# Two tiles of 256 tokens handed out with the sixth chunk, in a fused convolution and mixture-of-experts kernel

## The chip, the core and the metric

The kernel runs on one core of one Trainium2 chip. Its time is the device time of one execution in microseconds; the kernel before has a median of 1246.07 us over three runs (1243.16 to 1247.38). The profile comes from one more execution of the same program. TensorE (PE) multiplies matrices, VectorE (DVE) and ScalarE (ACT) work elementwise, GpSimd (POOL) computes a little and issues the indirect transfers, SyncE (SP) issues the other transfers. Each engine works through its own list of instructions in the order in which the program wrote them.

## The reference

```python
# x: (8, 3584, 192), weight_gen: (8, 3584, 8, 7)
w = softmax(weight_gen, over the last axis)           # 7 taps per token and head
x_unf[b, s, k] = x_pad[b, s + k]                      # 6 rows of zeros ahead of each sequence
out = einsum('bshk,bskhg->bshg', w, x_unf)            # a causal convolution, 8 heads of 24
# out as 28672 tokens of 192
logits = out @ w_gate                                 # 8 experts
e = argmax(logits); gate = softmax(logits)[e]
y = gate * (maximum(out @ w1[e], 0.0) @ w2[e])        # 192 -> 1024 -> 192, of one expert
```

Every token goes through the convolution, then through the one expert with the highest logit.

## The kernel before

The 28672 tokens are cut into 28 chunks of 1024, counted from 0 (`NCH`, `J * P`). For each chunk VectorE forms the convolution (`taps`, L354 and L378, fourteen passes over 128x1536); the result is split into a 16-bit high part (ScalarE, L448) and its residual (VectorE, `low`, L461 to L467). TensorE transposes the parts (L473), ScalarE copies them out (L475), TensorE forms the logits (`logits`, L485), VectorE the arg max and the gate (`route1`, `gate`), TensorE counts ranks (`ranks`, L512 and L514), VectorE turns them into places in eight queues in device memory, one per expert (`places`, L535 to L544), and POOL scatters the chunk's rows there with eight indirect transfers (`send`, L559). After the last chunk `pad_queues` scatters eight more, of padding rows. Behind a chunk, `choose` runs `select` (L573 to L605, on VectorE, one partition) for each event of the plan: it picks the experts whose queues are longest and writes the first rows of the tiles to be run.

A tile is T rows of one expert's queue. SP fetches it (`fetch`): its rows, transposed (`xt`, L743), all weights of its expert (`wt`, L745, 1796 KB, three buffers before the last chunk's tiles) and its gates (`meta`, L748). A tile's `xt` waits until its chunk's rows are in the queue; where the fetch stands in the program behind `pad_queues`, its `xt` waits for the padding rows too. On TensorE a tile is 8 blocks of the hidden layer, five matmuls each (L805, T columns wide; `fg` blocks in a group, two where T is 256, one where it is 384), and then for each 128 tokens 24 matmuls of the second layer (L711, 192 columns). Between the two the hidden values are split into `hh` and its residual `hl`. That goes one of two ways (L811): with ScalarE alone and a matmul that subtracts (L814, L818, L820), or with ScalarE and VectorE (L825, L828). A tile's second layer is written into the next tile's groups (`second`, `prev`).

What is handed out after which chunk is fixed when the program is written. `t_main` gives the sizes of tile for a chunk: nothing after chunk 0, 256 after chunks 1 to 4 (`EARLY` is 5), 384 after that, and 384, 256 and 128 after the last one. `make_plan` adds 1024 to `pending` with each chunk and hands out a tile of T while `pending > E * (T - 1)`, that is while some expert must have T rows in its queue. Before, that gives 1, 4, 4 and 4 tiles of 256 after chunks 1 to 4, none after chunk 5, three of 384 after chunk 6, two after chunk 7, three after chunk 8, three after chunk 9, two after chunk 10 and so on in this pattern, and after chunk 27 three of 384, three of 256 and 22 of 128 and fewer.

The order of the instructions is written by a planner with two clocks of its own, `clock[0]` for VectorE and `clock[1]` for TensorE. `vector_step` appends VectorE's next piece (a residual, a step of a chunk's routing, of its split, of the convolution) while VectorE's clock is behind TensorE's; then the next group of a tile is appended. A tile is not begun before its selection stands in the list, and TensorE's clock is put to at least `FETCH` = 16 after it (L977). With a chunk's split, its transposes go to TensorE's list at that place.

Of the kernel before, what the change touches and what calls it, by code (L numbers as in the profile page):

```python
# [20 lines left out]
E = 8  # L21
# [13 lines left out]
EARLY = 5  # L35
# [17 lines left out]
T_MAIN = 384  # L53
# [18 lines left out]


def t_main(c, last):
    if c < 1:
        return []
    if c < EARLY:
        return [256]
    if c < last:
        return [T_MAIN]  # L80
    return [T_MAIN, 256, 128]


def make_plan(n_chunks, chunk):


    events, pending = [], 0

    def full(ev, T):
        nonlocal pending  # L90
        s = 0
        while pending > E * (T - 1):
            pending -= T
            s += 1
        if s:
            ev.append((T, s, None))

    for c in range(n_chunks):
        pending += chunk
        ev = []  # L100
        for T in t_main(c, n_chunks - 1):
            full(ev, T)
        events.append(ev)


    T = 128
    n = (pending + E * (T - 1)) // T
    ends = [min(T, pending // k if k <= E else (pending - T * (k - E)) // E) for k in range(1, n + 1)]
    events[-1].append((T, n, [-(-m // T_STEP) * T_STEP for m in ends]))
    return events  # L110
# [3 lines left out]
def conv_moe_kernel(ctx: ExitStack, tc: tile.TileContext, x, wgen, w_gate, w1, w2, out):  # L114
# [4 lines left out]
    NCH = NP // J  # L119
# [488 lines left out]
    todo = []  # L608
# [109 lines left out]
    def fetch(n):  # L718
        T, rows, i, c, _ = todo[n]

        def rows_of(ins):


            for later in range(c + 1, sent[0] + 1):
                tc.declare_no_dep(ins.ins, group=f"s{later}", reason="the rows read were written by earlier chunks")
            for names in writers[:c + 1]:
                for name in names:
                    tc.add_manual_dep(ins.ins, name, wait_for, reason="may have written the rows read")
            tc.add_to_no_dep_group("qr", ins.ins)

        r = nc.sync.value_load(rows[0:1, i:i + 1], min_val=0, max_val=E * NCAP - 512)
        e = nc.s_assert_within(r >> 15, 0, E - 1,
                               skip_runtime_bounds_check_because="a row of queue e lies in [e * NCAP, (e + 1) * NCAP)")
        late = c == NCH - 1
        if late and not lates:

            conv_pools.close()
            lates.append(ctx.enter_context(tc.tile_pool(name="late", bufs=AHEAD, side="right", reuse_waits="tile")))
            lates.append(n)
        ring = late and (n - lates[1]) % (AHEAD + 3) < AHEAD  # L740
        px, pw = (lates[0], lates[0]) if ring else (ffx, ffw)
        xt = px.tile([P, 3, T_MAIN], F16, name="xt", bufs=AHEAD if ring else 3)
        rows_of(nc.sync.dma_start_transpose(xt[:, :, 0:T], q16[ds(r, T), 0:2 * D]))  # L743
        wt = pw.tile([P, WROW], F16, name="wt")
        nc.sync.dma_start(wt, wq[ds(e * P, P), :])  # L745
        meta = px.tile([P, 4, 2], F32, name="meta", bufs=AHEAD + 1 if ring else 4)
        p = min(P, T)
        rows_of(nc.sync.dma_start(meta[0:p, 0:T // p, :], q32[ds(r, T), D:D + 2].rearrange("(s p) c -> p s c", p=p)))  # L748
        return T, xt, wt, meta
# [4 lines left out]
    def experts():  # L754
# [8 lines left out]
        n = 0  # L763

        def second(m):
            while m > 0:
                r = next(prev, 0)
                if r == 0:
                    break
                if r is None:  # L770
                    m -= 1
                else:
                    outs.append(r)

        def flush():
            while outs:
                idx, o = outs.pop(0)
                scatter(out, idx, o, "o", bound=N - 1)

        while True:  # L780
            go = yield n, 0.0
            if not go:
                break
            while len(done_) < min(n + 2, len(todo)):
                loaded[len(done_)] = fetch(len(done_))
                done_.append(len(done_))
            T, xt, wt, meta = loaded.pop(n)

            fac = ffx.tile([P, 4], F32, name="fac", bufs=1)
            hh = ffh.tile([P, NF, T], F16, name="hh", padded_shape=[P, NF, T_MAIN])  # L790
            hl = ffh.tile([P, NF, T], F16, name="hl", padded_shape=[P, NF, T_MAIN])
            fg = max(g for g in (1, 2, 4, 8) if g * T <= 512 or g == 1)
            groups = NF // fg
            for t in range(groups):
                if t:
                    yield None, 0.0
                f0 = t * fg
                flush()
                while len(pend) > 3:
                    low_part()  # L800
                ph = ps_h.tile([P, fg, T], F32, name="ph")
                for g in range(fg):
                    f = f0 + g
                    for k, (wc, xc) in enumerate(((0, 0), (0, 2), (O_L0, 0), (O_H1, 1), (O_L1, 1))):
                        nc.tensor.matmul(ph[:, g], wt[:, wc + f * P:wc + (f + 1) * P], xt[:, xc, 0:T],  # L805
                                         start=(k == 0 and g == 0), stop=(k == 4),
                                         skip_group_check=g > 0)
                hv, lv = hh[:, f0:f0 + fg], hl[:, f0:f0 + fg]
                while subs:
                    subs.pop(0)()  # L810
                if (n % 3 == 1 or todo[n][3] < EARLY) and todo[n][3] < NCH - 1:  # L811


                    nc.scalar.activation(hv, ph, AF.Relu, scale=SHRINK)  # L814

                    def rest(ph=ph, hv=hv, lv=lv, fg=fg):
                        for g in range(fg):
                            nc.tensor.matmul(ph[:, g], negi, hv[:, g], start=False, stop=True,  # L818
                                             skip_group_check=True)
                        nc.scalar.activation(lv, ph, AF.Relu)  # L820

                    subs.append(rest)
                    clock[1] += T * fg * (6 + 4.5) / 2400.0 + 15 * fg * MM
                else:
                    nc.scalar.activation(hv, ph, AF.Relu)  # L825

                    def lo(ph=ph, hv=hv, lv=lv):
                        nc.vector.scalar_tensor_tensor(lv, ph, 0.0, hv, op0=ALU.max, op1=ALU.subtract)  # L828
                        return (T * fg + 60) / 960.0

                    cost = T * fg * (5 + 4.5) / 2400.0 + 14 * fg * MM
                    clock[1] += cost
                    pend.append((clock[1] + LATE, n, lo))
                if t > 0 or groups == 1:
                    while pend and pend[0][1] < n:
                        low_part()
                    m = -(-left // (groups - t))
                    second(m)
                    left -= m
                if t == groups - 1:  # L840
                    p = min(P, T)
                    nc.scalar.activation(fac[0:p, 0:T // p], meta[0:p, 0:T // p, 0], AF.Copy,
                                         scale=wt[0:p, O_INV:O_INV + 2].bitcast(F32))
                if t >= 1 and len(done_) < len(todo):
                    m = len(done_)
                    if m <= n + 2 or (todo[m][3] == NCH - 1 and m <= n + AHEAD + 2):
                        loaded[m] = fetch(m)
                        done_.append(m)
            while subs:
                subs.pop(0)()  # L850
            second(10 ** 6)
            prev = l2(T, hh, hl, wt, meta, fac)
            left = -(-T // P) * NF * 3
            n += 1
# [4 lines left out]


    plan = make_plan(NCH, J * P)
    clock = [0.0, 0.0]

    def low_part():
        at, _, lo = pend.pop(0)
        clock[0] = max(clock[0], at) + lo()
# [93 lines left out]
    with tc.manual_schedule(engines={mybir.EngineType.DVE}):  # L960
# [6 lines left out]
        n, _ = next(parts)  # L967
        while n is not None or parts is not None:
# [11 lines left out]
            n, _ = parts.send(True)  # L980
# [23 lines left out]
```

## Time and profile before

| | |
|---|---|
| median of three runs | 1246.07 us (1243.16 to 1247.38) |
| the profiled execution | 1242.18 us, span 1240.5 us |
| TensorE busy | 1133.4 us (91%), granted clock 0.965 |
| VectorE busy | 1036.7 us (84%) |
| ScalarE busy | 696.8 us (56%) |
| GpSimd busy | 660.6 us (53%) |
| weight loads (wt) | 97 of 1796 KB |
| read from and written to device memory | 239 GB/s over the span |

The busy times are means over stages that differ: up to about 175 us the expert weights are prepared and the first chunks run, then tiles and chunks go side by side until about 1020 us, and after that there are only tiles. So a stretch of the span tells more than the whole.

### The profile page before, as it was taken

How to read it: one execution, taken by the hardware profiler on the slowest of the kernel's cores; microseconds unless marked ns; L12 is line 12 of the kernel's file. 1: busy time of each engine (PE TensorE's matmuls, PEld its weight loads, DVE VectorE, ACT ScalarE, POOL GpSimd, SP SyncE). 2: the span in 40 equal slices, each digit the busy share in tenths (PEclk: the TensorE clock that was granted, in tenths of full speed). 3: DMA queues.
4: the chain of work that ended last, by engine and by line, in shares of the span. 5: the costliest groups of instructions: out<-in, count | busy, mean ns of one | idle time of the engine just before them, and what ended most of it. 6: DMA issues, size and time to landing. Idle time of an engine off the chain costs nothing.

```text
span 1240.5 us, 30087 instructions
## 1 busy us (share of the span) xinstructions
PE 1133.4 (91%) x11621; PEld 927.2 (75%) x11621; DVE 1036.7 (84%) x1849; ACT 696.8 (56%) x1459; POOL 660.6 (53%) x562
## 2 busy tenths in 40 slices
PE   5692189997999999999999999999999998999997
PEld 3461179896678788778788787787777786789997
DVE  7999966999999999999999999999998976232331
ACT  3455167675566666656756666656655663543442
POOL 6850853666656565446755565656464656222222
PEclk9896599999999999999999999999999999999998
DMA  9996698897768878787798878878776667999995
GB/s 277 346 323 241 232 282 264 287 304 236 232 201 267 265 230 250 238 234 235 247 277 237 237 227 255 247 240 254 239 215 178 191 197 222 340 348 348 321 362 218
DMA packets 185133, 320.93 MB, mean 259 GB/s; under 512 B 132752, under 2 KB 156434, under 8 KB 169118
## 3 DMA queue, kind: packets, MB, share of 16 engines
q1 hardware_dynamic: 162862, 273.68, 70.8%
q0 software_dynamic: 22128, 45.33, 11.1%
q8 instruction: 91, 1.49, 0.5%
q14 instruction: 52, 0.43, 0.1%
HBM read 236.17 MB, written 60.76 MB: 239 GB/s over the span
## 4 chain that ended last, share of the span: by engine, by line
PE 63%; DVE 13%; DMA 10%; issue 7%; POOL 4%; SPq 1%; ACT 1%; POOLq 0%; DVEq 0%; ACTq 0%
PE ph L805 29%; PE y L711 27%; DVE tv L354 4%; DVE acc L378 3%; DMA wt<-wq 3%; PE ph L473 2%; PE ph L818 2%; DMA f<-in_moe_w_dram 2%; POOL out_dram L559 2%; DMA xt<-queue 2%; DMA queue<-pl,pos 2%; DVE hl L828 1%; POOL queue L559 1%; PE ph L363 1%; PE pm L485 1%
## 5 line engine op out<-in xcount | busy, mean ns | idle before, releaser
L805 PE MATMUL ph<-xt,wt 128*128 128x384 f16 (+6 forms) x3880 | 578.8, 292 | 24.5 <-DMA wt<-wq 16.8
L711 PE MATMUL y<-wt,hh 128*128 128x192 f16 (+2 forms) x3696 | 504.5, 247 | 2.1 <-ACT o L715 2.1
L559 POOL DMA_INDIRECT out_dram<-o,meta x231 | 288.5, 1249 | 394.6 <-ACT o L715 349.0
L711 PE MATMUL y<-wt,hl 128*128 128x192 f16 (+2 forms) x1848 | 450.3, 247 | 0.4 <-ACT hl L820 0.2
L805 PEld LDWEIGHTS <-wt 128*128 128x128 f16 x3880 | 329.3, 98 | 144.4 <-DMA wt<-wq 18.9
L711 PEld LDWEIGHTS <-hh 128*128 128x128 f16 (+2 forms) x3696 | 337.0, 99 | 35.9 <-issue 5.0
L559 POOL DMA_INDIRECT queue<-pl,pos x224 | 286.8, 1280 | 118.1 <-issue 56.7
L828 DVE SCALAR_TENSOR_TENSOR hl<-ph,hh 128x384 f16<-128x384 f32 (+2 forms) x372 | 204.2, 562 | 144.2 <-ACT hh L825 139.0
L354 DVE TENSOR_TENSOR tv<-x_sb,wp 128x1536 f32<-128x1536 f32 (+1 forms) x171 | 289.0, 1693 | 3.9 <-PE ph L363 3.7
L825 ACT ACTIVATE hh<-ph 128x384 f16<-128x384 f32 (+2 forms) x372 | 185.5, 501 | 181.0 <-PE ph L805 170.4
L378 DVE TENSOR_TENSOR acc<-acc,tv 128x1536 f32<-128x1536 f32 x150 | 261.8, 1745 | 0.0
L711 PEld LDWEIGHTS <-hl 128*128 128x128 f16 (+2 forms) x1848 | 181.7, 98 | 16.5 <-ACT hl L820 1.4
L814 ACT ACTIVATE hh<-ph 128x384 f16<-128x384 f32 (+1 forms) x204 | 105.2, 518 | 84.7 <-PE ph L805 82.0
L715 ACT ACTIVATE o<-y,fac 128x192 f32<-128x192 f32 (+2 forms) x231 | 91.7, 418 | 89.4 <-PE y L711 83.4
L820 ACT ACTIVATE hl<-ph 128x384 f16<-128x384 f32 (+1 forms) x204 | 104.1, 519 | 37.0 <-PE ph L818 36.4
L475 ACT ACTIVATE xg<-ph 128x1024 f16<-128x1024 f16 x84 | 83.9, 1027 | 24.3 <-PE ph L473 24.2
L473 PE MATMUL ph<-idh,pl 128*128 128x128 f16 x672 | 56.1, 225 | 25.4 <-ACT pl L448 15.8
L818 PE MATMUL ph<-hh,negi 128*128 128x384 f16 (+1 forms) x256 | 68.1, 304 | 1.7 <-ACT hh L814 1.6
L473 PEld LDWEIGHTS <-pl 128*128 128x128 f16 x672 | 44.5, 101 | 29.4 <-ACT pl L448 16.1
L363 PE MATMUL ph<-tv,identf 128*128 128x384 f32 x126 | 51.6, 553 | 7.6 <-DVE tv L354 7.3
L413 ACT ACTIVATE junk<-x_sb 128x768 bf16<-128x768 f32 (+2 forms) x56 | 48.0, 857 | 13.6 <-DMA x_sb<-in_x_dram 6.5
L322 POOL TENSOR_TENSOR w_sb<-w_sb,mx 128x448 f32<-128x448 f32 x28 | 29.7, 1062 | 45.5 <-DVE mx L321 43.6
(121 smaller groups left out, 780.7 us busy)
## 6 DMA issues: line engine op xcount, KB each, us to landing
wt<-wq SPq DMA_DIRECT2D x97, 1796.0 KB
x_sb<-in_x_dram SPq DMA_DIRECT2D x27, 1344.0 KB
w_sb<-in_weight_gen_dram SPq DMA_DIRECT2D x28, 224.0 KB
wq<-ws SPq DMA_DIRECT2D x8, 772.0 KB
f<-in_moe_w_dram SPq DMA_DIRECT2D x8, 768.0 KB
f<-in_moe_w_dram SPq DMA_DIRECT2D x8, 512.0 KB
wq<-ws SPq DMA_DIRECT2D x8, 512.0 KB
wq<-ws SPq DMA_DIRECT2D x32, 128.0 KB
```

The source lines that it names most:

```text
L354: eng.tensor_tensor(out, xs, ws, op=ALU.mult)
L378: eng.tensor_tensor(ac, ac, t, op=ALU.add)
L473: nc.tensor.transpose(pt[:, m, :], p16[:, j, n * P:(n + 1) * P], idh)
L559: st = nc.gpsimd.indirect_dma_start(out=dst, out_offset=bass.IndirectOffsetOnAxis(ap=idx, axis=0), in_=src, in_offset=None, **kw)
L711: nc.tensor.matmul(y, hx[:, f, sl], w2v[:, f, t, :], start=(f == 0 and k == 0), stop=(f == NF - 1 and k == 2))
L715: nc.scalar.activation(o[0:m, :], y, AF.Copy, scale=fac[0:m, s:s + 1])
L805: nc.tensor.matmul(ph[:, g], wt[:, wc + f * P:wc + (f + 1) * P], xt[:, xc, 0:T], start=(k == 0 and g == 0), stop=(k == 4), skip_group_chec ...
L814: nc.scalar.activation(hv, ph, AF.Relu, scale=SHRINK)
L818: nc.tensor.matmul(ph[:, g], negi, hv[:, g], start=False, stop=True, skip_group_check=True)
L820: nc.scalar.activation(lv, ph, AF.Relu)
L825: nc.scalar.activation(hv, ph, AF.Relu)
L828: nc.vector.scalar_tensor_tensor(lv, ph, 0.0, hv, op0=ALU.max, op1=ALU.subtract)
```

## The change

Chunk 5 hands out at most two tiles of 256. `t_main` returns pairs of a size and the most tiles that may go out; the condition at L811 takes chunk 5's tiles along, so that both go the way with ScalarE alone.

```diff
     if c < EARLY:
-        return [256]
+        return [(256, 99)]
+    if c == EARLY:
+        return [(256, 2)]
     if c < last:
-        return [T_MAIN]
-    return [T_MAIN, 256, 128]
+        return [(T_MAIN, 99)]
+    return [(T_MAIN, 99), (256, 99), (128, 99)]
...
-    def full(ev, T):
+    def full(ev, T, most):
         nonlocal pending
         s = 0
-        while pending > E * (T - 1):
+        while s < most and pending > E * (T - 1):
             pending -= T
             s += 1
...
-        for T in t_main(c, n_chunks - 1):
-            full(ev, T)
+        for T, most in t_main(c, n_chunks - 1):
+            full(ev, T, most)
...
-                if (n % 3 == 1 or todo[n][3] < EARLY) and todo[n][3] < NCH - 1:
+                if (n % 3 == 1 or todo[n][3] <= EARLY) and todo[n][3] < NCH - 1:
```

## Rows read from the trace of the kernel before

**Rows 1.** Busy time by stretch (start:end, length, engines, granted clock, DMA share, GB/s).
```profile
287.70:296.40 8.70, 5.56 (x69) 4.95 (x67) 8.30 (x15) 4.65 (x11) 7.13 (x5) 1.00 0.55 174
296.40:303.00 6.60, 6.47 (x58) 4.48 (x58) 6.60 (x13) 3.98 (x10) 2.12 (x2) 1.00 0.97 321
303.00:317.00 14.00, 8.48 (x68) 5.50 (x69) 14.00 (x25) 6.72 (x10) 9.76 (x7) 0.63 1.06 318
317.00:331.30 14.30, 13.58 (x128) 10.52 (x126) 14.30 (x30) 8.44 (x21) 7.49 (x6) 1.00 0.50 151
331.30:345.70 14.40, 13.04 (x118) 10.15 (x117) 14.40 (x25) 7.24 (x16) 8.93 (x8) 1.00 0.83 253
345.70:650.00 304.30, 304.26 (x3037) 242.58 (x3035) 297.57 (x529) 191.85 (x418) 174.14 (x139) 1.00 0.79 244
...
1021.00:1048.30 27.30, 23.93 (x218) 18.82 (x216) 20.81 (x66) 10.74 (x25) 20.90 (x22) 1.00 0.66 219
1048.30:1240.50 192.20, 184.82 (x2312) 168.36 (x2312) 52.20 (x84) 78.96 (x176) 46.40 (x48) 0.97 0.96 320
```

**Rows 2.** Chain of waits, 215 to 345 us (start, length, what).
```profile
215.26 12.71 DMA wt<-wq
...
261.84 1.09 PE ph L805 x10
...
265.50 1.99 PE y L711 x24
...
268.58 7.53 DMA wt<-wq
...
288.39 1.67 DVE acc L378
...
334.52 0.48 DVE hl L828
335.04 0.97 PE ph L805 x5
...
341.16 2.44 PE ph L805 x15
```

**Rows 3.** Chain of waits, 1041 to 1050 us.
```profile
1041.61 2.41 DMA queue<-padrow,padi
1044.04 4.10 DMA xt<-queue
1048.28 1.99 PE ph L805 x8
```

**Rows 4.** Timeline of TensorE (start, length, line, tiles, shape, [idle before]).
```profile
296.36 1.14 PE L805 MATMUL ph<-xt,wt 128*128 128x384 f16 x6 [2.32 <-DMA xt<-queue]
...
306.37 0.29 PE L473 MATMUL ph<-idh,pl 128*128 128x128 f16 x1 [3.50 <-ACT pl L448]
...
345.75 0.98 PE L805 MATMUL ph<-xt,wt 128*128 128x384 f16 x5
...
529.76 0.61 PE L473 MATMUL ph<-idh,pl 128*128 128x128 f16 x8
```

**Rows 5.** Timeline of VectorE, end of chunk 14's split.
```profile
529.59 0.14 DVE L467 TENSOR_TENSOR lsc<-isx,nin 128x1 f32<-128x1 f32 x1
```

**Rows 6.** Timeline of SP's queue, 292 to 323 us.
```profile
292.95 1.35 SPq L743 DMA_TRANSPOSE xt<-queue  x1
...
322.17 1.31 SPq L743 DMA_TRANSPOSE xt<-queue  x1
```

**Rows 7.** Timeline of POOL, first of chunk 7's eight rows.
```profile
306.51 0.99 POOL L559 DMA_INDIRECT queue<-pl,pos  x1 [2.70 <-DVE pos L544]
```

**Rows 8.** Groups by line and shape (count, busy us, mean ns, idle before).
```profile
L828 DVE SCALAR_TENSOR_TENSOR hl<-ph,hh 128x384 f16<-128x384 f32 x323 | 171.5, 546 | 65.5 <-ACT hh L825 65.3
...
L584 DVE TENSOR_TENSOR eq<-cand,top 1x128 f32<-1x128 f32 x7 | 2.0, 280 | 0.0
```

## The prediction

> **What bounds the kernel now.** I read the table by stretches first [rows 1], then the chain of waits in order of time [rows 2, 3], then single engines' timelines where the chain changes hands [rows 4 to 7], and last the prices by shape [rows 8]. Chunks are counted from 0, so the sixth is chunk 5; tiles are counted from 0 too.
>
> From 345.7 to 650 us TensorE is busy for 304.26 of 304.30 us, and after 1048.3 it has the work alone (184.8 of 192.2 us, VectorE 52.2) [rows 1]. VectorE in the first of these stretches is idle for only 304.30 - 297.57 = 6.7 us. So the middle is bound by both engines at once, and the end by TensorE. The two are locked by one written order: chunk 14's residual is ready on VectorE at 529.73 (529.59 + 0.14), and its transposes start on TensorE at 529.76 [rows 4, 5]. TensorE cannot run ahead of VectorE there by more than the order has put ahead of such a point.
>
> The hole lies before that. Tiles 9 to 12 belong to chunk 4, chunk 5 hands out nothing, and tile 13 waits for chunk 6: its xt is issued at 292.95, its first matmul runs at 296.36 [rows 4, 6]. In the five stretches from 287.7 to 345.7 TensorE idles 3.14 + 0.13 + 5.52 + 0.72 + 1.36 = 10.9 us, and the granted clock is 0.63 in the third (303 to 317), so part of it ran at the 1.2 GHz level [rows 1]. But from 288.4 to 335.0 the chain goes through VectorE [rows 2], which is busy all 42.7 us of the stretches from 303 on [rows 1]. TensorE's hole is therefore not simply time of the end.
>
> There is a second hole at the end of the middle. Tile 67's xt waits for the last padding row of the queues (1041.61 + 2.41), lands, and TensorE starts at 1048.28; in that stretch it idles 27.30 - 23.93 = 3.4 us [rows 1, 3].
>
> **The change part by part.** *What the plan hands out.* Before a chunk, pending tokens are compared with 8*(T-1). Chunk 4 leaves 1792; chunk 5 makes that 2816, over 2040, so two tiles of 256 go out and 2304 are left. Chunk 6 then has 3328 and hands out one tile of 384 in place of three, chunk 7 three in place of two, chunk 8 three as before, chunk 9 two in place of three; from there the pattern 3, 3, 2 stands one chunk off. Tokens handed out by chunk 6: 256 fewer; by chunks 7 and 8: 128 more, and so on by turns. The last chunk gets two tiles of 384 and four of 256, where it had three and three. In all 98 tiles instead of 97.
>
> *Prices on TensorE.* A 256-wide matmul costs 1.09/10 = 0.109 us, a 384-wide one 2.44/15 = 0.163, one of the second layer 1.99/24 = 0.083 [rows 2]. A tile of 256 is 40 x 0.109 + 48 x 0.083 = 8.3 us, and 9.2 with the eight residual matmuls of the ScalarE path; a tile of 384 is 40 x 0.163 + 72 x 0.083 = 12.5, and 13.8 with them. The edited condition (<= EARLY) puts both new tiles on the ScalarE path. Two tiles of 384 become three of 256, the same columns; 120 x 0.109 - 80 x 0.163 is nothing, and the ScalarE path costs 2 x 0.9 for the new tiles, less 1.3, since 18 instead of 19 of the 384-wide tiles take it: +0.5 us.
>
> *Prices on VectorE.* Residuals by VectorE before the last chunk: 37 tiles, before and after, so none gained or lost. One selection more: nine instructions whose dearest is 280 ns [rows 8], about 2.0 us, less some 0.4 for chunk 6's, which picks one tile instead of three: +1.6 us, on the chain in that stretch. Against it, before chunk 9's transposes only one tile (15) has its residuals on VectorE where two (14, 15) had: 8 x 0.546 = 4.4 us later [rows 8]. So VectorE reaches that point 2.8 us sooner, and must make it up later, where it has the 6.7 us of idle time.
>
> *One weight load more* (1.8 MB) stands in the stretch from 276 to 298 us. Loads took 7.5 to 12.7 us to land [rows 2]. The new tile 13's can go when tile 10 is done with its buffer, near 276, and lands between 284 and 289, while TensorE is with tile 12 until 287.7: hidden, or 1 us late. The three loads after it come one per freed buffer; at 12.7 instead of 9.2 us they would cost up to 3.5 us each, at 7.5 nothing. I take 1 us in all, since the nearest row (268.58) took 7.5. Should the cover go, this is the rival below that ends slower. The Trainium skill, "DMA: Bandwidth & Descriptors", section "Issuing engines are not separate DMA queues", says that transfers of SP and POOL share the same engines and interleave. The rows bear it out: the DMA share is 1.06 in 303 to 317 [rows 1]. By that rule the added load is not free there: at 318 GB/s it takes 5.6 us of all engines, and if all of it delayed chunk 6's rows, the sum below would come to nothing.
>
> *Where the filled time goes.* After tile 12 the plan had 13.8 + 2 x 12.5 = 38.8 us of tiles to run before chunk 7's first; now 2 x 9.2 + 12.5 = 30.9, which is 7.9 us less. The hole is filled at chunk 6 and opens again at chunk 7. Chunk 7's first xt was issued at 322.17 and needs about 3.4 us (292.95 to 296.36) [rows 4, 6]; with the added selection that is 327. TensorE starts on the new tiles at 288; with 30.9 us of tiles and about 4 us of transposes, logits and the like (345.75 - 287.7, less 38.8 of tiles, 10.9 of idle and up to 4.2 that the low clock cost, below), it gets there near 323 and waits some 4 us. It then runs chunk 7's first tile at 327, where that started at 345.75 [rows 4]: 18.7 us sooner with 7.9 us less done, a lead of 11. But that lead meets chunk 9's transposes, which hang on VectorE. What is kept is only what the written order has placed ahead of such points, and that follows from the tokens: in the end 128 more before the padding rows, 128 fewer after them.
>
> *The sum at the end.* Behind the padding rows the last chunk has 2 x 12.5 + 4 x 8.3 = 58.2 us of wide tiles instead of 3 x 12.5 + 3 x 8.3 = 62.4: -4.2. In front of them TensorE has 4.2 us more, covered by the idle 3.4 at 1044.9 and by the hole at 290. The time at which the padding rows land moves by -2.8 (VectorE, above) to +4 (1.6 of selection, 0.5 of TensorE, 1 to 2 of late loads); most of the 2.8 is made up later, so I take -0.3. Sum: -4.5 us, or 1237.7 for the profiled execution (1242.18, of which 1240.5 is its span). That execution lies 3.9 under the median of the three runs, so the forecast is 1246.07 - 4.5 = 1241.6.
>
> **Rivals.** *B, the whole hole is won.* VectorE is no lock: it idles less once TensorE is early, and the lead of 11 us lasts to the end. For it: VectorE's 6.7 us of waits in 345.7 to 650 come from TensorE being late. Against it: the transposes start within 0.1 us of their data [rows 4, 5]. Time: 1246.1 - 11 = 1235. The clock is part of that lead: 0.63 over 14 us means that some 10 us ran at the lower level, and the 8.5 us busy there cost up to 4.2 [rows 1]. The Trainium skill, "TensorE: Matmul & The Clock Gate", section "The HAM clock gate", says that the clock falls after idling and comes back with work; the rows agree, since the low clock follows idle 3.50 us [rows 4]. By that rule a wait near 323 could lower it anew, and B would be 1239.
>
> *C, nothing comes of it.* The order is locked, the hole moves by one chunk, and the padding rows land 4 us later, because VectorE has its 1.6 us more and the chunks' new phase brings other small waits. Then -4.2 is eaten: 1246.
>
> *D, slower.* TensorE used the hole to catch up: tile 13 is taken when it is free. Now the two tiles stand in the order ahead of chunk 7's ranks and chunk 8's transposes, and in POOL's queue tile 13's and 14's output scatters stand ahead of chunk 7's rows, which POOL began at 306.51 after waiting only for VectorE [rows 7]. If the three loads take 12.7 us, TensorE is 3 x 3.5 = 10.5 us late there; chunk 7's rows go out that much later, VectorE, which is the chain, stands, and the hole at chunk 7 grows. Of 10.5, the 2.8 are slack: +8, less 4.2: 1250. It decides from 4.2 + 2.8 = 7 us of lateness on. Against it: tiles 9 to 12 already ran like this, and right behind them, in 287.7 to 345.7, VectorE idled only 8.70 - 8.30 = 0.4 us [rows 1].
>
> **How the numbers follow.** Forecast 0.45 (its own range 1239 to 1244), B 0.15, C 0.22, D 0.18. About 0.3%, 3.7 us, is what can be told from no change: below 1242.3 is faster. Two thirds of the forecast's chance and all of B lie there: 0.45. The rest of the forecast and most of C: 0.35. D and the edge of C: 0.20. The range goes from B to D, 1235 to 1250.
>
> **What would show it.** Right: two tiles of 256 start between 287 and 300; the idle of TensorE before 306 is gone and 3 to 6 us stand before chunk 7's first tile, near 325; the granted clock no longer falls at 305; chunk 9's transposes start 0 to 4 us before 348; the idle ahead of the tile that waits for the padding rows shrinks under 2 us, and from there to the end it takes 188 us, not 192. Wrong: chunk 7's rows leave POOL after 312 (D); the tile of the padding rows starts at 1048 or later (C); it starts before 1040 (B). If the last stretch is not 4 us shorter, the sum itself is wrong.

## The result, and the profile after

The changed kernel takes 1250.88 us (median of 16 runs, 1245.77 to 1254.06), the kernel before 1242.09 us (16 runs beside it). The ratio is 1.0074, with a 95% interval from 1.0060 to 1.0088: the change costs some 9 us. The forecast was 1241.6 us and faster by 4.5; the time lies just outside the range, on its slow side. The forecast started from a median of three runs, 1246.07, which is 4.0 us above that of the 16, so against the kernel beside it the change was missed by some 13 us and not by 9. The profiled execution of the changed kernel took 1252.21 us (span 1250.5), that of the kernel before 1242.18 (span 1240.5).

From line 75 on, all lines of the changed kernel stand three further down: L805 of before is L808 here. The first view is the table by stretches, with the columns of [rows 1] (the engines in the order TensorE's matmuls, its weight loads, VectorE, ScalarE, POOL) and the same stretches up to 650; then comes the collision described below, and at the end the stretches up to and from the tile that waits for the padding rows.

```profile
287.70:296.40 8.70, 7.61 (x85) 6.91 (x83) 7.77 (x13) 6.30 (x15) 7.38 (x5) 1.00 0.56 150
296.40:303.00 6.60, 4.01 (x45) 3.62 (x42) 6.60 (x12) 3.12 (x8) 4.65 (x4) 0.96 0.96 365
303.00:317.00 14.00, 13.99 (x130) 11.86 (x131) 10.03 (x21) 8.29 (x17) 5.39 (x5) 0.90 0.64 252
317.00:331.30 14.30, 11.99 (x146) 10.14 (x143) 13.35 (x22) 6.85 (x12) 8.16 (x8) 1.00 0.62 201
331.30:345.70 14.40, 12.49 (x101) 8.87 (x101) 13.60 (x24) 7.23 (x19) 3.50 (x3) 0.88 0.91 245
345.70:650.00 304.30, 298.69 (x2933) 236.84 (x2934) 298.12 (x533) 189.76 (x409) 176.23 (x142) 0.99 0.80 242
676.00:698.00 22.00, 18.25 (x175) 14.31 (x173) 15.82 (x22) 13.02 (x26) 13.07 (x11) 0.92 0.73 236
1021.00:1059.90 38.90, 38.88 (x384) 30.68 (x382) 24.48 (x83) 20.92 (x46) 29.76 (x31) 1.00 0.68 219
1059.90:1250.50 190.60, 178.64 (x2282) 165.03 (x2282) 54.65 (x88) 74.48 (x167) 46.49 (x48) 0.98 0.97 322
```

The reader is to see two things. In the third stretch, where TensorE idled 5.52 us and its clock was 0.63 [rows 1], it is now busy for 13.99 of 14.00 us at 0.90. But VectorE, which had no idle time there, now stands for 14.00 - 10.03 = 4.0 us, and VectorE was the chain [rows 2]. And the last stretch begins at 1059.9 where it began at 1048.3, and is 1.6 us shorter, not 4.2.

**What stood in the way at 303 to 312.** The queue of SP (start, length, line, what):

```profile
274.82 1.32 SPq L746 DMA_TRANSPOSE xt<-queue  x1
...
277.79 0.34 SPq L748 DMA_DIRECT2D wt<-wq  x1
...
293.12 1.33 SPq L746 DMA_TRANSPOSE xt<-queue  x1
294.78 0.36 SPq L748 DMA_DIRECT2D wt<-wq  x1
```

The xt at 293.12 is tile 15's, which must wait for chunk 6's rows. The weights of tile 14, whose own rows were asked for at 274.82, stand behind it in SP's list and are issued only at 294.78, though the last matmul that used their buffer (tile 11's, L714) ended at 289.73. What follows shows in the timelines of four engines (start, length, engine, line, [idle before, and what ended it]):

```profile
290.82 0.94 PE L808 MATMUL ph<-xt,wt 128*128 128x256 f16 x7 [1.09 <-DMA wt<-wq]
...
303.01 0.39 PE L808 MATMUL ph<-xt,wt 128*128 128x256 f16 x1 [2.60 <-DMA wt<-wq]
...
332.52 1.77 PE L808 MATMUL ph<-xt,wt 128*128 128x384 f16 x7 [3.54 <-DMA xt<-queue]
...
349.52 0.23 PE L476 MATMUL ph<-idh,pl 128*128 128x128 f16 x1 [4.24 <-ACT pl L451]
...
305.70 0.60 ACT L817 ACTIVATE hh<-ph 128x512 f16<-128x512 f32 x1 [4.38 <-PE ph L808]
...
311.40 1.57 ACT L451 ACTIVATE pl<-acc 128x768 f16<-128x768 f32 x2
...
312.27 0.69 DVE L464 TENSOR_TENSOR pl<-acc,pl 128x512 f16<-128x512 f32 x1 [2.80 <-ACT pl L451]
...
310.39 1.00 POOL L562 DMA_INDIRECT out_dram<-o,meta  x1 [7.48 <-ACT o L718]
311.69 0.96 POOL L562 DMA_INDIRECT queue<-pl,pos  x1 [0.30 <-issue]
```

Read from the top: the two new tiles start at 290.82 and 303.01, each after a wait for its weights; the hole has moved to 332.52, ahead of chunk 7's first tile. Read on: ScalarE stands 4.38 us because tile 14 is late, chunk 8's high part (L451) stands in ScalarE's list behind tile 14's groups, VectorE waits for it at 312.27, and POOL holds back chunk 7's eight rows, because an output scatter that waits for tile 13's `o` stands ahead of them. They leave at 311.69, where before they left at 306.51 [rows 7]. Chunk 8's logits reach VectorE at 325.9 us instead of 317.8, and chunk 17's still 4.5 us later than before.

**A second place, which no step of the prediction had named.** Around 683 us all four engines stand. The chain of waits runs through it (start, length, what):

```profile
671.78 0.13 DVE pos L547
671.91 0.53 DVE mx L324
...
673.77 5.40 DMA queue<-pl,pos
...
684.27 1.12 POOL queue L562
685.41 1.00 POOL w_sb L325
...
686.91 0.47 ACT hl L823
```

The same place in the timelines:

```profile
673.77 0.97 POOL L562 DMA_INDIRECT queue<-pl,pos  x1 [0.30 <-DVE sm L335]
...
685.41 0.99 POOL L325 TENSOR_TENSOR w_sb<-w_sb,mx 128x448 f32<-128x448 f32 x1
...
686.43 0.58 ACT L328 ACTIVATE w_sb<-w_sb 128x448 f32<-128x448 f32 x1 [4.58 <-POOL w_sb L325]
...
687.44 0.22 PE L476 MATMUL ph<-idh,pl 128*128 128x128 f16 x1 [3.65 <-ACT hl L823]
...
695.79 0.56 DVE L831 SCALAR_TENSOR_TENSOR hl<-ph,hh 128x384 f16<-128x384 f32 x1 [6.17 <-ACT hh L828]
```

VectorE finishes the places of chunk 17 (L547) and right after them the maximum of chunk 20's tap weights (L324, ends at 672.4). So POOL's list has chunk 17's eight scatters first and then the subtraction of that maximum (L325), one instruction of 0.99 us. It starts at 685.41, 13.0 us after its data were ready. ScalarE's list has the exponential of the result (L328) ahead of a tile's `hl`: ScalarE stands 4.58 us, TensorE 3.65, VectorE 6.17. Chunk 18's logits are 11.5 us later than before, chunk 27's 12.1. In the kernel before, chunk 20's subtraction came ahead of the scatters, 0.1 us after its maximum. But chunk 27's came behind them there, in the timeline of before:

```profile
924.32 0.97 POOL L559 DMA_INDIRECT queue<-pl,pos  x1 [2.21 <-DVE pos L544]
...
936.62 0.97 POOL L322 TENSOR_TENSOR w_sb<-w_sb,mx 128x448 f32<-128x448 f32 x1
...
937.62 0.58 ACT L325 ACTIVATE w_sb<-w_sb 128x448 f32<-128x448 f32 x1 [3.63 <-POOL w_sb L322]
```

So the collision was there once before too, late in the span, and in the new order it stands at chunk 20, where more stands behind it; chunk 27's subtraction starts 1.5 us after its maximum there. A late subtraction alone is no loss: chunk 6's starts 11.6 us after its maximum before and 11.4 in the change, and no idle time of ScalarE stands ahead of its exponential.

**The account.** From VectorE's first look at chunk 7's logits (288.1 us before, 288.6 after) to the last padding row's issue is 753.5 us before and 764.7 after: +11.2. From there to the end it is 198.9 and 197.2: -1.7. With the 0.5 ahead of chunk 7 that makes the 10.0 us between the spans.

### The profile page after: what moved, and what is told of

Same layout as the page of the kernel before. It is cut to its first block, busy times and chain, and to the rows that moved or that the text cites. A ratio compares the mean times of both kernels' runs of the same rounds, so it can differ in the third digit from the quotient of the medians.

```text
span 1250.5 us, 30197 instructions
## 1 busy us (share of the span) xinstructions
PE 1140.5 (91%) x11669; PEld 936.8 (75%) x11669; DVE 1040.5 (83%) x1854; ACT 696.6 (56%) x1456; POOL 663.9 (53%) x562
## 3 DMA queue, kind: packets, MB, share of 16 engines
q0 software_dynamic: 22128, 45.33, 11.2%
q8 instruction: 91, 1.49, 0.5%
## 4 chain that ended last, share of the span: by engine, by line
PE 64%; issue 11%; DVE 9%; DMA 8%; POOL 6%; ACT 1%; SPq 1%; POOLq 0%; DVEq 0%; ACTq 0%
PE ph L808 31%; PE y L714 27%; DMA wt<-wq 4%; POOL out_dram L562 3%; PE ph L821 2%; PE ph L476 2%; DVE tv L357 2%; DVE acc L381 2%; DMA queue<-pl,pos 1%; POOL queue L562 1%; PE pm L488 1%; DVE hl L831 1%; DMA w_sb<-in_weight_gen_dram 1%; DMA wq<-ws 1%; DMA f<-in_moe_w_dram 1%
## 5 line engine op out<-in xcount | busy, mean ns | idle before, releaser
L808 PE MATMUL ph<-xt,wt 128*128 128x384 f16 (+7 forms) x3920 | 580.5, 292 | 29.9 <-DMA wt<-wq 24.4
L562 POOL DMA_INDIRECT out_dram<-o,meta x231 | 296.8, 1285 | 421.5 <-ACT o L718 372.6
L714 PE MATMUL y<-wt,hh 128*128 128x192 f16 (+2 forms) x3696 | 503.9, 247 | 0.1
L714 PE MATMUL y<-wt,hl 128*128 128x192 f16 (+2 forms) x1848 | 451.1, 247 | 0.2
L808 PEld LDWEIGHTS <-wt 128*128 128x128 f16 x3920 | 334.3, 98 | 149.3 <-DMA wt<-wq 27.1
L714 PEld LDWEIGHTS <-hh 128*128 128x128 f16 (+2 forms) x3696 | 337.8, 99 | 36.8 <-issue 5.3
L562 POOL DMA_INDIRECT queue<-pl,pos x224 | 281.8, 1258 | 103.3 <-issue 54.9
L714 PEld LDWEIGHTS <-hl 128*128 128x128 f16 (+2 forms) x1848 | 181.9, 99 | 14.5 <-ACT hl L823 0.8
L451 ACT ACTIVATE pl<-acc 128x768 f16<-128x768 f32 (+1 forms) x53 | 41.1, 820 | 18.5 <-DVE acc L381 15.3
```

Of the source, the lines that this page charges most:

```text
L562: st = nc.gpsimd.indirect_dma_start(out=dst, out_offset=bass.IndirectOffsetOnAxis(ap=idx, axis=0), in_=src, in_offset=None, **kw)
L714: nc.tensor.matmul(y, hx[:, f, sl], w2v[:, f, t, :], start=(f == 0 and k == 0), stop=(f == NF - 1 and k == 2))
```

## The experiments

The expectations name their theories by letters. P: the subtraction behind the scatters in POOL's list costs most of it (in a_sub20, P20: chunk 20's alone; P11: chunk 11's as well). W: the weights of tile 14 behind tile 15's xt, and the lists of ScalarE and POOL behind these, cost most of it. In a_dep and a_dep_sub, S is the order in SP's list and L the added load itself. In b_ph, O is that the order alone moves the time and N that it does not. In a_tail and b_tail, B is that weight loads set the pace of the end, so that fewer columns there save little, and T is that TensorE sets it. Ratios are to runs of the kernel before made beside each group of kernels (their medians are 1241.01 to 1242.72), so they are not quotients of the column of medians; the brackets are 95% intervals, from 6 to 16 runs of a kernel in five rounds. "Middle" is the time from chunk 7's logits to the last padding row in that run's one profile, "end" what is left behind it; these two come from one execution each.

| kernel | median, us | ratio | middle | end |
|---|---|---|---|---|
| before | 1242.09 | 1 | 753.5 | 198.9 |
| the change | 1250.88 | 1.0074 [1.0060, 1.0088] | 764.7 | 197.2 |
| a_sub | 1244.24 | 1.0017 [1.0004, 1.0029] | 756.4 | 195.8 |
| a_sub20 | 1244.93 | 1.0018 [0.9997, 1.0038] | 757.5 | 196.4 |
| a_nowt | 1244.89 | 1.0016 [0.9999, 1.0033] | 760.3 | 197.2 |
| a_dep | 1248.75 | 1.0057 [1.0037, 1.0076] | 761.2 | 196.3 |
| a_dep_sub | 1240.52 | 0.9994 [0.9975, 1.0013] | 754.2 | 196.1 |
| a_late | 1241.74 | 1.0002 [0.9988, 1.0016] | 753.9 | 198.5 |
| a_one | 1240.36 | 0.9985 [0.9970, 1.0000] | 756.0 | 194.0 |
| a_one_sub | 1236.40 | 0.9963 [0.9949, 0.9977] | 754.2 | 194.4 |
| a_tail | 1248.65 | 1.0058 [1.0039, 1.0077] | 766.0 | 190.6 |
| b_sub | 1238.62 | 0.9969 [0.9957, 0.9982] | 752.5 | 198.3 |
| b_ph | 1239.16 | 0.9978 [0.9962, 0.9994] | 751.3 | 198.8 |
| b_tail | 1239.78 | 0.9989 [0.9977, 1.0001] | 754.0 | 195.8 |

**a_sub: the subtractions of chunks 11 and 20 on VectorE.** Chunk 11's is the other one that made ScalarE stand for over 4 us in the change (it came 7.8 us late, behind output scatters).

```diff
-        nc.gpsimd.tensor_tensor(k.w, k.w, ..., op=ALU.subtract)
+        (nc.vector if c in (11, 20) else nc.gpsimd).tensor_tensor(k.w, k.w, ..., op=ALU.subtract)
```

> The changed kernel, but the subtraction of the maximum for chunks 11 and 20 runs on VectorE and not on GpSimd, so that ScalarE's exponential cannot wait behind GpSimd's scatters there (near 345 and 683 us in its trace). Theory P (GpSimd's list: the moved order put these two subtractions behind scatters, and ScalarE, then TensorE and VectorE, stood): 8 to 10 us faster than the change, so at the kernel before or up to 2 us under it; chunk 18's logits reach VectorE at about +4 instead of +11.5 us against before. Theory W (the two tiles come too late for the order, weights and all, before chunk 9): stays at the change's time within 2 us, since the loss is there by 320 us.

The ratio fell from 1.0074 to 1.0017, with intervals apart: some 7 us of the 9 are gone. P holds for the larger part; by W the time would have stayed within 2 us of the change.

**a_sub20: chunk 20's alone.**

```diff
+        (nc.vector if c in (20,) else nc.gpsimd).tensor_tensor(k.w, k.w, ..., op=ALU.subtract)
```

> The changed kernel with chunk 20's subtraction alone on VectorE (chunk 11's stays on GpSimd). Theory P20 (the collision at 683 us is what a_sub won): 5 to 6 us faster than the change, 1245. Theory P11 (the one at 345 us counts too): 2 to 3 us faster than the change, the rest was chunk 11's.

1.0018: chunk 20's subtraction does all that the two did, and chunk 11's counted for nothing that can be measured, though ScalarE stood 4.68 us there in the change and 4.35 here. ScalarE's exponential in the timeline of this kernel follows the subtraction at once, and POOL's scatters hold nobody:

```profile
670.36 0.58 ACT L328 ACTIVATE w_sb<-w_sb 128x448 f32<-128x448 f32 x1 [0.23 <-DVE w_sb L325]
...
670.96 0.97 POOL L562 DMA_INDIRECT queue<-pl,pos  x1 [0.30 <-DVE rowc L576]
...
682.17 1.12 POOL L562 DMA_INDIRECT queue<-pl,pos  x1 [0.30 <-DMA queue<-pl,pos]
```

The middle is 7.2 us shorter than in the change (764.7 - 757.5), as the medians say.

**b_sub: the same in the kernel before, for its own late subtraction, chunk 27's.**

```diff
+        (nc.vector if c in (27,) else nc.gpsimd).tensor_tensor(k.w, k.w, ..., op=ALU.subtract)
```

> The kernel before, but the subtraction for chunk 27 runs on VectorE; in its trace this one subtraction also waits behind eight scatters (12.1 us after its maximum, near 937 us), and ScalarE idles 3.6 us for it, TensorE 1.6. Theory P: 2 to 3 us faster than the kernel before. Theory W: no change within 1 us.

0.9969, with an interval that lies below 1: one subtraction of 0.63 us moved to VectorE makes the kernel before some 4 us faster than it was, more than the 2 to 3 that were expected. Its one profile shows less of it: from chunk 24's logits to chunk 25's it gains 1.7 us on the kernel before, and the middle is 1.1 shorter; where the rest comes from is not shown. In its timeline it runs right behind its maximum, where before it started at 936.62:

```profile
924.41 0.62 DVE L321 TENSOR_REDUCE mx<-w_sb 128x64 f32<-128x448 f32 x1
925.07 0.63 DVE L322 TENSOR_TENSOR w_sb<-w_sb,mx 128x448 f32<-128x448 f32 x1
```

**a_nowt: tile 14 uses tile 13's weights.** Its load is left out, so tile 14 is computed with another expert's weights.

```diff
-        wt = pw.tile([P, WROW], F16, name="wt")
-        nc.sync.dma_start(wt, wq[ds(e * P, P), :])
+        wt = lwt[13] if n == 14 else pw.tile([P, WROW], F16, name="wt"); lwt[n] = wt
+        nc.sync.dma_start(wt, wq[ds(e * P, P), :]) if n != 14 else 0
```

> The changed kernel, but the second new tile (14) loads no weights of its own and uses tile 13's; that one load is left out. Theory W: tile 14 starts at once after tile 13 (298 instead of 303 us), chunk 7's rows leave GpSimd 4 to 5 us sooner, chunk 8's logits come at +3 instead of +8 against before, and the time falls by 4 to 5 us. Theory P: the collision near 683 us stays, and the time falls by less than 2 us.

1.0016, some 7 us less than the change, with intervals apart: more than W's 4 to 5, and not P's under 2. Tile 14 starts at 296.2 instead of 303.0, and chunk 7's rows leave POOL when they did before [rows 7]:

```profile
305.15 1.06 POOL L562 DMA_INDIRECT out_dram<-o,meta  x1 [3.08 <-ACT o L718]
306.52 0.96 POOL L562 DMA_INDIRECT queue<-pl,pos  x1 [0.30 <-DVE pos L547]
```

Chunk 17's logits are 3.2 us ahead of before (in the change 4.5 behind); then chunk 20's subtraction comes 14.2 us late, ScalarE stands 5.83, and chunk 18's are 6.1 behind. So the late load is a cause of its own, and the collision takes 9 us at one stroke even from a kernel that is ahead. A load less is also a transfer less, so this run alone gives no price for the place of the load in the list. And since leaving out the load and moving the subtraction (a_sub20) regain some 7 of the same 9 us each, the two costs do not simply add; no run has both.

**a_dep: the order in SP's list.** Tile 15's xt waits until tile 14's weights have landed, so those go first.

```diff
-        rows_of(nc.sync.dma_start_transpose(xt[:, :, 0:T], q16[ds(r, T), 0:2 * D]))
+        xi = nc.sync.dma_start_transpose(xt[:, :, 0:T], q16[ds(r, T), 0:2 * D]); rows_of(xi); tc.add_manual_dep(xi.ins, wts[n - 1], wait_for, reason='order') if n == 15 else 0
...
-        nc.sync.dma_start(wt, wq[ds(e * P, P), :])
+        wts[n] = nc.sync.dma_start(wt, wq[ds(e * P, P), :]).ins.name
```

> The changed kernel with one swap in SyncE's list and no other: tile 15's xt, which waits for chunk 6's rows, stands behind tile 14's weights and not ahead of them (it waits for them to land). Theory S (SyncE's list: the weights of the second new tile went out at 294.8 only because the xt ahead of them waited for chunk 6's rows until 293.1, though their buffer was free near 290): they go out at 289 to 291, tile 14 starts at 298 to 299 instead of 303.0, the time falls by 3 to 5 us, and all but the collision near 683 us is gone by chunk 17. Theory L (the load itself: there is no time for it between tile 11's end and tile 14, whatever stands ahead): it lands little sooner, the time falls by less than 1.5 us, and leaving the load out, which gave 6, was worth that for the load's own time.

SP's queue in this kernel:

```profile
280.62 0.34 SPq L748 DMA_DIRECT2D wt<-wq  x1
...
292.63 0.34 SPq L748 DMA_DIRECT2D wt<-wq  x1
...
302.49 1.36 SPq L746 DMA_TRANSPOSE xt<-queue  x1
304.16 0.35 SPq L748 DMA_DIRECT2D wt<-wq  x1
```

1.0057, against 1.0074 for the change: 2 us, between S (3 to 5) and L (under 1.5), and the intervals overlap. This execution was 3.3 us late at chunk 7 already, so distances tell more: tile 14 starts 9.4 us behind tile 13 (12.2 in the change), and from chunk 7 to chunk 17 the logits lose 0.6 us against before (4.0 in the change). From there on the collision costs as much as in the change. The weights go out at 292.63, 12 us behind those of tile 13, as soon as their buffer is free (292.52 here); in the change the list held them back by 5.0 us beyond that, which made tile 14 some 2.8 us later. But the edit does more than swap the two: the xt now waits until the weights have landed and goes out at 302.49 instead of 293.12, tile 15's own weights at 304.16 instead of 300.31, and TensorE waits 1.11 us for these at 313.56. So the order may be worth more than this run shows.

**a_dep_sub: both mended.** The edits of a_dep, and chunk 20's subtraction on VectorE.

```diff
+        xi = nc.sync.dma_start_transpose(...); rows_of(xi); tc.add_manual_dep(xi.ins, wts[n - 1], wait_for, reason='order') if n == 15 else 0
...
+        (nc.vector if c in (20,) else nc.gpsimd).tensor_tensor(k.w, k.w, ..., op=ALU.subtract)
```

> The swap in SyncE's list and chunk 20's subtraction on VectorE together, in the changed kernel. Theory S with theory P: the two losses are separate and add, 3 to 5 and 5 to 6 us, so 1239 to 1243, at or under the kernel before. Theory L with P: as with the subtraction alone, 1244.

0.9994: all of the loss is gone. That is what S and P foretold together. The middle is 754.2 us, against 753.5 before, and by the profiles some 7.2 of the 10.5 us regained are the subtraction's (a_sub20), some 3.5 the list's (a_dep). And nothing is gained: with both accidents out of the way, the change is worth 0.7 us, inside its interval, and not the 4.5 of the forecast. Even that flatters it, since the kernel before still has its own collision, at chunk 27. Against b_sub, where that one is mended (0.9969), this kernel is some 3 us slower, with intervals that just overlap.

**a_late: another order of the same work.** The planner's clock for TensorE is put 5 us later when it comes to the first new tile; nothing else is edited.

```diff
-                clock[1] = max(clock[1], todo[n][4] + FETCH)
+                clock[1] = max(clock[1], todo[n][4] + FETCH) + (5.0 if n == 13 else 0.0)
```

> The changed kernel, but the planner is told that the first new tile begins 5 of its us later, so that more of VectorE's list (chunk 7's places, chunk 8's split) stands ahead of the two tiles in the order; nothing is computed otherwise. Theory W: chunk 7's rows leave GpSimd at 307 and not at 311.7, chunk 8's logits come at +3 instead of +8 against before, and by chunk 17 the kernel is 3 to 5 us ahead of the change. Theory P alone: the same loss as in the change until chunk 17, and what comes later follows from whether a subtraction waits behind scatters.

1.0002. What was hoped for at chunk 8 didn't come: tile 14's weights still stand behind tile 15's xt, tile 14 starts at 305.5, and chunk 8's logits are 9.0 us later than before (8.0 in the change; 3.1 and 0.5 of these were there at chunk 7). But now chunk 20's subtraction falls ahead of chunk 17's scatters, and the middle is 753.9:

```profile
671.53 0.98 POOL L562 DMA_INDIRECT out_dram<-o,meta  x1 [0.30 <-issue]
672.51 1.01 POOL L325 TENSOR_TENSOR w_sb<-w_sb,mx 128x448 f32<-128x448 f32 x1
```

So it is the order alone that brings the collision, not the two tiles as such. And the 6.0 us that this kernel loses between chunks 7 and 8 are mostly made up: by chunk 17 it is 4.7 - 3.1 = 1.6 us.

**a_one: one tile of 256 after chunk 5.**

```diff
-        return [(256, 2)]
+        return [(256, 1)]
```

> One tile of 256 with the sixth chunk instead of two. Theory W: only one tile stands ahead of chunk 7's rows and chunk 8's transposes, the loss by chunk 9 is under 3 us where it was 4 to 6, and the time lies between the two kernels or under the one before. Theory P: the order moves anew, and the time follows from whether ScalarE waits for GpSimd's subtraction more than 3 us anywhere after 340 us; without such a wait it is at or under the kernel before.

0.9985, its interval just reaching no change. The hole is filled in part (TensorE waits 5.61 us at 299.19), the subtraction collides here too, and still the end is 4.9 us shorter than before (28 weight loads are issued behind the padding rows, where it was 29; what that is worth by itself is not shown):

```profile
683.88 2.21 POOL L562 DMA_INDIRECT queue<-pl,pos  x1 [0.30 <-issue]
686.12 0.97 POOL L325 TENSOR_TENSOR w_sb<-w_sb,mx 128x448 f32<-128x448 f32 x1
```

**a_one_sub: one tile, and chunk 20's subtraction on VectorE.** This is the version that the runs pointed to.

```diff
-        return [(256, 2)]
+        return [(256, 1)]
...
+        (nc.vector if c in (20,) else nc.gpsimd).tensor_tensor(k.w, k.w, ..., op=ALU.subtract)
```

> One tile of 256 with the sixth chunk, and chunk 20's subtraction on VectorE, which in the run with one tile waited 12.3 us behind scatters (ScalarE idle 3.5 us). Theory P: 3 to 5 us faster than with one tile alone, so about 1236, under both kernels. Otherwise 1240.

0.9963 [0.9949, 0.9977], 1236.40 us: the fastest of all, ahead of both kernels. Its interval overlaps that of b_sub, so whether the one tile adds anything to the mended subtraction stays open.

**b_ph: the kernel before in another order.** Other tiles take the way with ScalarE alone (one in three as before, but the next of the three).

```diff
-                if (n % 3 == 1 or todo[n][3] < EARLY) and todo[n][3] < NCH - 1:
+                if (n % 3 == 2 or todo[n][3] < EARLY) and todo[n][3] < NCH - 1:
```

> The kernel before with the same plan and the same number of tiles on each path, but the ScalarE path goes to tiles with n % 3 == 2 and not 1: a new order of the list and no change of work. Theory O (what the change lost after chunk 17 is luck of the order): the time moves by 2 to 8 us either way, up where a subtraction waits behind eight scatters with ScalarE idle for over 3 us, down where none does after 345 us. Theory N (order alone is harmless): within 2 us of the kernel before.

0.9978 [0.9962, 0.9994]. No subtraction after 345 us makes ScalarE stand for more than 2.04 us here, and chunk 20's runs well ahead of the scatters:

```profile
668.11 0.96 POOL L322 TENSOR_TENSOR w_sb<-w_sb,mx 128x448 f32<-128x448 f32 x1 [3.46 <-DVE mx L321]
```

A phase that changes no amount of work moves this kernel by 0.2%, or 2.7 us. That is on O's side, but the interval reaches down to 0.7 us, where N has its under 2.

**a_tail and b_tail: one load less at the end.** Tile 86 of the change uses tile 85's weights, tile 85 of before tile 84's; the load is left out, and that tile is computed with another expert's weights.

```diff
-        wt = pw.tile([P, WROW], F16, name="wt")
-        nc.sync.dma_start(wt, wq[ds(e * P, P), :])
+        wt = lwt[86-1] if n == 86 else pw.tile([P, WROW], F16, name="wt"); lwt[n] = wt
+        nc.sync.dma_start(wt, wq[ds(e * P, P), :]) if n != 86 else 0
```

In b_tail the 86 is 85.

> The changed kernel, but tile 86 (128 tokens, among the last chunk's) loads no weights of its own and uses tile 85's; TensorE's work and order, and those of every engine but SyncE, are as in the change. Theory B (after the padding rows the weight loads set the pace: 30 loads before and after the change, so the 4.2 us of TensorE work that went had little to take with it): one load less, 5 to 6 us at the 340 GB/s of that stretch, so the time from the tile that waits for the padding rows to the end falls from 190.6 to 185 to 187, and the run by 3 to 5 us. Theory T (TensorE sets the pace there, as the prediction had it): under 1 us.

> The kernel before with one load less in the same place (tile 85 uses tile 84's weights). Theory B: 1.5 to 5 us faster, its idle time before the last tiles (1.6 us before tile 96) gone. Theory T: under 1 us, and a gain only after the change, if there.

TensorE's waits from the tile of the padding rows to the end (engine, line, what it waited for, us in total, times, longest). The first view is the change, the second a_tail, where those for weights are gone, and the third the kernel before, from which b_tail takes this one away:

```profile
PE ph L808 <- DMA wt<-wq: 4.9, 4, 2.2
PE ph L808 <- DVE hl L831: 1.3, 1, 1.3
```

```profile
PE ph L808 <- DVE hl L831: 1.3, 1, 1.3
PE ph L808 <- ACT hh L817: 0.4, 1, 0.4
```

```profile
PE ph L805 <- DMA wt<-wq: 1.6, 1, 1.6
```

From that tile to the end, a_tail takes 183.5 us (the change 190.6), b_tail 189.0 (before 192.2). The profiles are on B's side: a load costs more in the change's tail (7.1 us, where B had 3.6 to 5.6) than in that of before (3.2). The medians are not as clear: a_tail 1.0058 against 1.0074, with overlapping intervals, b_tail 0.9989, with an interval that reaches past 1. That TensorE waits for loads at places is shown; how much one is worth at the end is not.

## Why the prediction was wrong

**Right.** The plan came out as counted (98 loads, one tile fewer of 384 and one more of 256 behind the last chunk). The hole before 306 is mostly filled: in the first three stretches TensorE idles 3.7 us instead of 8.8. The clock in the third is 0.90 instead of 0.63, though it still fell, to 0.50 from 303 to 305 us behind the wait of 2.60, where the forecast had no fall. The hole reopens at chunk 7: 3.54 us, within the 3 to 6 that were forecast, with the tile behind it at 332.5 (forecast 327). That the wait's length fits is in part luck: TensorE came to it at 329.0 instead of 323, so both of its ends are late by some 6 us. The idle 3.4 us ahead of the padding rows' tile is gone, too (38.88 of 38.90 us busy). In B, a new wait was to lower the clock anew by the Trainium skill's "TensorE: Matmul & The Clock Gate", section "The HAM clock gate": the trace agrees, with 0.55 from 333 to 335 us, right behind that wait, and 0.88 in the stretch that begins with its end. Chunk 9's transposes start at 349.5, which is 1.5 us outside the 344 to 348 that were forecast.

**The step that failed first** is "the time at which the padding rows land moves by -2.8 (VectorE, above) to +4 (1.6 of selection, 0.5 of TensorE, 1 to 2 of late loads) ... so I take -0.3". It moved by +11.8: the xt that waits for them was at 1044.04 [rows 3] and is at 1055.80. The -2.8 of VectorE in it is not what failed: with tile 14's load left out (a_nowt) the logits do gain 2.7 us between chunks 7 and 17, in one execution. That sum priced engine work and loads only, and took the order of the lists as harmless. The missing term is the order. In POOL's list, chunk 20's subtraction fell behind eight scatters: 7 us, shown by a_sub and a_sub20, and by a_late, where another order does the same. In SP's list, the second load fell behind an xt that had to wait: some 2 to 3.5 us, by a_dep and the difference of a_dep_sub and a_sub20. There the intervals overlap, so by the times this second part is not beyond doubt; the traces show the 5.0 us for which the load was held back. No rival had the first of these; it could have been read from before's own trace, where chunk 27's subtraction starts 12.1 us late in the same way.

**Late loads**, taken at "1 us in all", measured 1.09 and 2.60 us of TensorE's time for the new tiles; the second is the list's doing, since no such wait stands ahead of tile 14 in a_dep. The term was too small all the same: without tile 14's load (a_nowt) the middle is 4.4 us shorter and the time some 7. The sum's sentence on the added transfer (the Trainium skill, "DMA: Bandwidth & Descriptors", section "Issuing engines are not separate DMA queues") had the added load delay chunk 6's rows by up to 5.6 us (1796 KB at 318 GB/s, an estimate). The trace does not bear that price out: chunk 6's last scatter ends at 291.4 us instead of 288.7, but chunk 5's, ahead of the added load, ended 2.5 us later too.

**The second step that failed is the -4.2 of the tail.** It measured -1.6. TensorE's busy time from the padding rows' tile on did fall by 184.82 - 178.64 = 6.2 us, but its idle time rose by 4.6: 190.60 - 178.64 = 12.0 against 7.4 [rows 1]. The waits shown with a_tail and b_tail make up all of it: those for weights went from 1.6 to 4.9 us, and one of 1.3 for `hl` came. Behind the padding rows 29 loads are issued before and after, and they run at the same rate. The rows below are the part of the tail with loads, first the change and then before (columns of [rows 1]):

```profile
1059.90:1230.00 170.10, 165.99 (x2061) 153.16 (x2062) 53.38 (x85) 70.08 (x155) 42.06 (x43) 0.99 1.05 342
```

```profile
1048.30:1230.00 181.70, 180.13 (x2278) 164.26 (x2279) 52.20 (x84) 77.84 (x173) 44.68 (x46) 0.99 1.02 338
```

With the DMA share at 1.05 and 342 GB/s, against 1.02 and 338, the same loads were not done sooner, and 3.3 of the 6.2 us that TensorE saved became waiting for them. The prediction counted this tail as bound by TensorE alone, since VectorE was idle there; it didn't look at the share of the DMA engines in the same row [rows 1].

**Rival D** had the direction, and its mechanism is in the trace, 0.3 us short of its mark (chunk 7's rows left at 311.69, the mark was after 312). It is right by a third at most: its 8 us would have come from lateness at chunk 7, which a_late shows to be mostly made up by chunk 17. That the time came out near its 1250 is luck: another cause of 7 us stood in its place, and its 1250 was counted from 1246.07, so from 1242.09 it would have been 1246. C's four microseconds of "other small waits" were the same idea too small. Of the forecast's gain nothing is left even when both accidents are mended (a_dep_sub).

What stays open: whether the order of SP's list is worth 2 or 3.5 us, or more; what tile 14's load costs by itself; what a load is worth in the tail; and whether handing out one tile early gains anything over the kernel before with its subtraction mended. Segments of a profile come from single executions, which differ by up to 3.4 us either way ahead of chunk 7.

## What to carry to other kernels

Where a change makes a planner write another order, follow each engine's list across the seam and look for a cheap instruction behind a batch of slow ones or behind a wait: one subtraction of 1 us behind eight scatters cost 7 us here, more than the 4.5 that the whole change was meant to gain, and moving it to an engine with room won them back. Look for such accidents in the trace of before first, and price a new order as an uncertainty of its own (here 0.2% down in b_ph, 0.6% up for the one subtraction). And a stretch counts as bound by an engine only once its DMA share has been read as well.

## What the runs showed of the hardware

Eight indirect scatters, issued by POOL back to back, held its list from 673.77 to 685.39 us, 1.45 us each on average, though most are 0.96 long: single ones lasted 2.05 or 1.49 us, and 0.30 lies between any two. A wait of 4.58 us on ScalarE behind them, of 3.65 on TensorE and 6.17 on VectorE became 7 us at the end, nearly undiminished over the 565 us that follow, while the 6.0 us lost at chunk 8 in a_late had shrunk to 1.6 by chunk 17. Which late pieces are made up was not to be told from the idle time alone: chunk 11's subtraction made ScalarE stand for 4.68 us at no measurable cost.
